# Ten gathered attention tiles: one value product each in place of two, and another set of constants for the order

## The chip, the cores and the metric

The kernel runs on one core of a Trainium2 chip. The metric is the device time of one execution in microseconds (us); lower is better. A measurement of this kernel is the median of several executions. Beside these there is a profile of one execution, with the start and the duration of each instruction on each engine.

The engines are TensorE (PE, with its weight loads as PEld), VectorE (DVE), ScalarE (ACT), GpSimd (POOL) and SyncE (SP). SP's queue carries most of the DMA transfers.

## The reference

Sparse attention over `B, H, S, D = 4, 8, 768, 64`, followed by a feed-forward layer of 512 to 2048 to 512 with a squared ReLU:

```python
scores = scale * np.matmul(q, k.transpose(0, 1, 3, 2))
mask = np.abs(blk_i - blk_j) <= 1            # blocks of 32 positions, 24 of them
mask = mask | (blk_i == 0) | (blk_j == 0) | (blk_i == n_blocks - 1) | (blk_j == n_blocks - 1)
...                                          # and three sampled key blocks for each query block
attn = softmax(np.where(mask, scores, -1e9))
x = np.matmul(attn, v)                       # heads side by side: 3072 x 512
r = np.maximum(x @ w_in, 0.0)
out = (r * r) @ w_out
```

The first and the last query block see all keys; each other block sees its neighbours, the two edge blocks and its three sampled blocks.

## The kernel before

Everything lies in one program without loops. Python functions issue the instructions of single steps, and a planner inside the kernel decides, when the program is built, in which order they are issued.

**Batches 0 and 1** are computed densely, with a mask. A unit is a pair of heads (four units for each batch). Q and K come in as f32, are cast to bf16 (`cast_qk`), transposed by PE (`transp`, `transp_pe`) and copied to `QK` (`evac`, with the helper `copy` at L289 and L291). A score visit (`scores`, L513 and L517) uses half of the array's rows for each head. Then follow `exps` on ACT (L524), the mask product on DVE (`masks`, L531), the value products (`values`, L553), `normalize`, a transpose back (L570) and a copy into `xT`.

**Batches 2 and 3** are computed in gathered tiles, six for each batch, in the order `SEQ` = 5, 0, 1, 2, 3, 4. A tile holds four blocks of queries (tile 5 holds two, and beside them the two edge blocks that see all keys). Keys are gathered by DVE and ACT copies within SBUF. Values are written to DRAM (`vd`) and come back as a window (`v_window`, SP, L704) and as sampled blocks (`v_random`, POOL's indirect DMA, L714) into one of two buffers, which the profile names `RAW` and `MK` after the memory that they share. For each tile of four blocks there are two scores (`s_scores`, L726), one for each pair of head pairs, two `s_exps` (L738), and then the value products (`s_values`, L772), which write 32-row strips of one accumulator `ab`. `s_normalize`, `s_transp` (L788) and `s_evac` bring the result into `xT`.

**The feed-forward layer** runs beside the attention. `hidden` (L821) multiplies `xT` by `w_in`; `relu` (ACT L830 or DVE L832) and `square` (POOL L843 or ACT L841) give `g`; `output` (L871) multiplies by `w_out`; `out_copy` and `store` write the result.

**The order.** Each step is a `Task` with the engines that may run it, an estimated duration, the tasks that it depends on, the buffers that it takes (`get`) and frees (`put`), a key, and a time `after` before which the planner doesn't start it. `run_schedule` always takes the task that can start first by its own clock, and among equals the one with the lowest key. A small pseudo-random number, drawn from `SEEDS` and scaled by `TIES`, is added to each key. Tasks with keys of 100 and more (the feed-forward layer, casts for later batches, gathered tiles that are late in the list) may go ahead of a key under 100 on the same engine only where they could start more than `AHEAD` sooner. The due times come from these constants:

- `PACE0`, `PACE` and `VISITS`: the score visits of batch 1, one entry of `VISITS` for each
- `LEAD`: the casts of Q and K for batch 1, against the visits
- `TILE_AT`: the scores of the twelve gathered tiles; `SLEAD` us before that their gathers may begin
- `EARLY`: the loads of the eight units of batches 2 and 3
- `NB_`: how far the keys of the gathered batches are spread
- `PATIENCE`, `KACT`: how long the planner holds back for a score visit, and how much it prefers DVE for a gather

The scores of all batches, and the value products too, are chained in one fixed sequence, so a due time only counts where it is later than those ahead of it. The planner knows nothing of the chip but its own estimates; what the chip runs is the order of instructions on each engine that comes out.

Of the kernel before, what the change touches and what calls it, by code (L numbers as in the profile page):

```python
# [25 lines left out]
def kernel(  # L26
# [62 lines left out]
    OVER = {"PE": 0.0, "DVE": 0.08, "ACT": 0.09, "POOL": 0.03, "SP": 0.0}  # L89
    SWITCH, HEAD, SLACK = 0.096, 0.14, 0.1  # L90
    SEGMENT, FETCH = 256, 4.6
    AHEAD = {"PE": 0.055, "DVE": 0.075, "ACT": 0.127, "POOL": 0.0, "SP": 0.0}
    LEAD = -4.055
    NB_, SLEAD, KACT = 78.318, 3.363, 0.3
    EARLY = (-37.337, -571.032, -447.965, 102.579, 109.844, 58.537, 96.246, 21.479)
    TILE_AT = (-87.603, 9.262, 99.097, 156.639, -2.44, 142.415, 182.155, 190.828, 133.068, 169.829, 174.13, 84.9)
    VISITS = (8.112, -135.256, -11.672, -92.97, -64.857, -395.022, 12.104, -192.992, -90.327, 19.791, -173.633, -177.084, -46.108, -63.873, -62.087, -15.727, 6.189, 16.892)
    HOLD, PATIENCE = 0, 20.357
    PACE0, PACE, SINGLE, MASK_AT = 45.988, 1.334, 1, 17.0

# [2 lines left out]
    class Buf:  # L105
        def __init__(self, pool):
# [2 lines left out]

    TIES = 2.072, 7.892
    SEEDS = (
            371417, 510513, 591591, 260703, 130052, 619188, 398403, 547159, 30476,
            318629, 58182, 18274, 283039, 791673, 964966, 267641, 668336, 10009,
            208115, 562447, 518448, 450915, 243995, 901117)

# [14 lines left out]
    class Task:  # L134
        def __init__(self, engs, key, fn, deps=(), get=(), put=(), after=0.0, mode=None, dma=0.0, late=None, bias={}, port=False,
# [8 lines left out]
            self.order = len(tasks)  # L144
            self.key += TIES[0 if key < 300 else 1] * tie(self.order)
            for b in self.put:
# [745 lines left out]
    def T_(engs, key, f, *args, **kw):  # L892
        return Task(engs, key, (lambda e: f(*args, e)), **kw)
# [132 lines left out]
    def attend_sparse(b):  # L1026
        us = range(b * HP, (b + 1) * HP)
        keys = [ev[u][1, 0] for u in us]
        qrs = [ev[u][0, 0] for u in us]
        vals = [x for u in us for x in cv[u]]  # L1030
        base = N1 + (b - ND) * NB_
        wr = T_(("SP", 0.6), base - 5, vd_write, b, deps=vals + sp0, dma=2.1)
        xs_first = True
        for p_ in range(NT):
            t = SEQ[p_]
            n = len(blocks_of(t))
            seq = STILES.index((b, p_))
            x = seq % 2
            s = base + p_ * NB_ / NT
            kb, vb = Buf("KG"), Buf("VG")  # L1040
            over = {0: lambda: [y for u in range(ND * HP) if raw_set(u) == 2 for y in cv[u] + tr[u]], 1: lambda: []}[x]() if seq < 2 else []
            vover = ([y for u in range(ND * HP) if raw_set(u) == 3 for y in cv[u] + tr[u]] if x == 0 else mks) if seq < 2 else []
            deps = []
            late = TILE_AT[seq]
            if p_ in PLACES:
                ts = SEQ[p_:PLACES[p_]]
                kp = T_(("DVE", 1.5), s - 8.1, k_places, ts, deps=sp0 + k_last[-1:], after=late - SLEAD - 2.0)
            k1 = T_({"DVE": 0.43, "ACT": 0.61}, s - 8, k_window, b, t, x, list(range(n))[:2], deps=keys + over + k_first[-1:], get=[kb],
                    after=late - SLEAD, port=True, nop=2, bias={"ACT": KACT})
            deps.append(k1)  # L1050
            k_first.append(k1)
            if n > 2:
                deps.append(T_({"DVE": 0.43, "ACT": 0.61}, s - 8, k_window, b, t, x, [2, 3], deps=[k1], port=True, nop=2, bias={"ACT": KACT}))
            if p_ < 2:
                deps.append(T_(("DVE", 0.8 if p_ == 0 else 0.49), s - 8, k_global, b, x, p_ == 0, deps=[k1] + kg_all[-1:], port=True, nop=2))
                kg_all.append(deps[-1])
            for qs_ in ([0, 1], [2, 3])[:n // 2]:
                deps.append(T_(("DVE", 1.2), s - 8, k_random, b, t, x, qs_, deps=[k1, kp] + sp0, port=True, nop=6))
            k_last.append(deps[-1])
            deps.append(T_({"DVE": 0.6, "POOL": 1.27}, s - 8, q_tile, b, t, x, deps=qrs + [k1] + qz, after=late - SLEAD, port=True, nop=2))  # L1060
            v1 = T_(("SP", 1.1), s - 8, v_window, b, t, x, deps=[wr] + vover + v_first[-1:], get=[vb], dma=0.38 * n, after=late - SLEAD)
            vdeps = [v1]
            v_first.append(v1)
            if p_ < 2:
                vdeps.append(T_(("SP", 1.8), s - 8, v_global, b, x, deps=[v1], dma=1.0))
            for i in range(n):
                vdeps.append(T_(("POOL", 1.05), s - 8, v_random, b, t, x, i, deps=[v1] + sp0, dma=0.48, late=5.5, quiet=True))
            pairs = [(0, 1), (2, 3)] if n == 4 else [(a,) for a in range(HP)]
            ab = Buf("X2")
            va = None  # L1070
            groups = [[g_] for g_ in pairs] if n == 4 else [pairs[0:2], pairs[2:4]]
            for k_, grp in enumerate(groups):
                end = k_ == len(groups) - 1
                us_sc, nm_ = (0.47, 16) if n == 4 else (0.46, 10)
                exs, pts = [], []
                for j, g_ in enumerate(grp):
                    sb_ = Buf("X2")
                    sc = T_(("PE", us_sc), s, s_scores, b, t, x, g_, sb_, deps=deps + sc_all[-1:], get=[sb_],
                            put=[kb] if end and g_ == grp[-1] else [], mode=128, after=late, paced=True, mm=nm_)
                    sc_all.append(sc)  # L1080
                    pt = Buf("pT")
                    pts.append(pt)
                    ex = T_(("ACT", 1.02), s, s_exps, b, t, g_, deps=[sc], get=[pt], put=[sb_])
                    if t in (0, NT - 1):
                        ex = T_({"DVE": 0.09 * len(g_), "POOL": 0.15 * len(g_)}, s - 1, s_patch, b, t, g_, deps=[ex])
                    exs.append(ex)
                    for u in us:
                        sc_of[u].append(sc)
                va = T_(("PE", 0.245 if n == 4 else 0.5), s + 2.6 * NB_ / 36, s_values, b, t, x, grp, ab, deps=exs + vdeps + va_all[-1:],
                        get=[] if k_ else [ab], put=pts + ([vb] if end else []), mode=32, mm=32 if n == 4 else 64)  # L1090
                va_all.append(va)
                for u in us:
                    va_of[u].append(va)
            xb_ = Buf("xs")
            nm = T_(("DVE", 0.95), s - 9, s_normalize, b, t, deps=[va], get=[xb_])
            kw = {}
            if b not in xb:
                xb[b] = Buf("xT")
                kw = dict(get=[xb[b]])
            xt = T_(("PE", 0.24), s - 9, s_transp, b, t, deps=[nm], put=[xb_], mode=128, mm=4)  # L1100
            mu["s", b, p_] = T_({"DVE": 0.47, "ACT": 0.56}, s - 9, s_evac, b, t, p_, deps=[xt], put=[ab], **kw)
# [4 lines left out]
    sc_all, va_all, ob = [], [], {}  # L1106
    mr = []
    for i, (c0, c1) in enumerate(((0, QW), (QW, S))):
        rb_ = Buf("X1")
        t = T_(("PE", 0.11 + 0.11 * i), 5.0 if i else -90.0, mask_rows, c0, c1, rb_, after=9.8 if i else 4.6, get=[rb_], put=[], mode=32, mm=1)  # L1110
# [6 lines left out]
    for us in [range(b * HP, (b + 1) * HP) for b in range(B)]:  # L1117
# [8 lines left out]
        if us[0] < HP:  # L1126
            for c0, c1, at in MASKED:
                for n in range(NCH):
                    mb, w = Buf("X1"), (c1 - c0) / 512
                    t = T_(("PE", 0.216 * w), (2 * n + 30 if c0 == 0 else 2 * n + 2), mask_tile, n, c0, c1, mb, get=[mb], mode=128, after=at, deps=mr, mm=1)  # L1130
                    x = T_({"DVE": 0.15 + 0.53 * w, "ACT": 0.22 + 0.37 * w}, (2 * n + 30 if c0 == 0 else 2 * n + 2), mask_evac, n, c0, c1, deps=[t], put=[mb])
                    for c in range(c0, c1, P):
                        mk[n, c] = x
        while mine:
            n = min(len(mine), GROUPS[us[0] // HP][mine[0][1] // QW])
            if n == 3:
                n = sum(a[:2] == mine[0][:2] for a in mine)
# [8 lines left out]
    for k_, T in enumerate(TILES + [None]):  # L1146
# [4 lines left out]
        for _, kind, x in sorted(both, key=lambda z: z[:2]):  # L1151
            n_key += 1
            t = x[0]
            b, c0, w = t
            if kind == 0:
# [9 lines left out]
                for part in range(parts):  # L1165
                    end = part == parts - 1
                    hd.append(T_(("PE", HID[w] / parts), n_key - (0.6 if part else 0.5), hidden, t, f, part, parts, hb,
                                 deps=hd[-1:] or need + [wl[f * NWP // NF], wl[(f + per_unit(t) - 1) * NWP // NF]],
                                 get=[] if part else [hb], put=[xb[b]] if last_use and end else [], mode=128, mm=per_unit(t) * KM // parts, yields=not part and pool == "X2"))
# [3 lines left out]
                n = 1 if wide else per_unit(t)  # L1173
# [3 lines left out]
            else:  # L1177
                _, i, part = x
                ts, cs = y_tiles(t)[i]
                n = (cs[1] - cs[0]) / d_model  # L1180
                fs = range(part * NF // NY, (part + 1) * NF // NY)
                if part == 0:
# [3 lines left out]
                        deps=[sq_of[t, f] for f in fs] + [wl[NWP + f * NWP // NF] for f in fs] + ([yprev] if part else []),  # L1186
                        get=[] if part else [yb], put=[gbuf[t, f] for f in fs if (t, f) in gbuf] if last_i else [], mode=128, mm=NF // NY)
# [39 lines left out]
```

## Time and profile before

| | |
|---|---|
| median of 3 runs | 271.44 us (271.15 to 272.69) |
| the profiled execution | 271.15 us, of which 269.2 are the profile's span |
| busy share of the span | PE 96%, ACT 74%, DVE 60%, POOL 54% |
| granted TensorE clock | full, mean 1.00 |
| data read from HBM and written to it | 37.62 MB and 8.03 MB |

The profiled time is the time of the whole execution; the span runs from the first to the last instruction that the profile shows. All times of instructions below are counted from the start of the span. "L871" is line 871 of the kernel, "x16" is a count of instructions, and an entry such as `[0.16 <-issue]` tells how long the engine stood idle just before a group and what ended that. The "chain that ended last" is followed back from the last instruction: at each step to what released it, or to the instruction before it on its engine.

### The profile page before, as it was taken

The page shows a single profiled execution, that of the slowest core. Times are in us where ns is not written, and L with a number is a line of the kernel's source. Part 1 is how long each engine was busy: PE and PEld are TensorE (multiplying, and loading weights), DVE is VectorE, ACT ScalarE, POOL GpSimd, SP SyncE. Part 2 cuts the span into 40 slices and gives each one's busy share as a digit, 9 for nine tenths or more (in the row PEclk, how much of TensorE's full clock was granted, in tenths as well). Part 3 has the DMA queues.
Part 4 walks back from the last instruction along what each step waited for, and adds up shares of the span by engine and source line. Part 5 has one row for each costly group of instructions (what it writes and reads, how often), then busy time and mean ns, then how long its engine had stood idle before and what let it go on. Part 6 is the DMA issues. An engine that isn't in the chain of part 4 may idle for free.

```text
span 269.2 us, 8933 instructions
## 1 busy us (share of the span) xinstructions
PE 259.4 (96%) x3658; PEld 170.6 (63%) x3696; DVE 161.2 (60%) x465; ACT 199.9 (74%) x304; POOL 146.4 (54%) x185
## 2 busy tenths in 40 slices
PE   8999999989999999999999999999999999999995
PEld 6778876667676746665766556655675666545544
DVE  7898898989898689899535464361444723301010
ACT  3897989988989799888975549845878876714821
POOL 4292915765971410468886771762288975712520
PEclk9999999999999999999999999999999999999999
DMA  6999999955511025669769681326453372321022
GB/s 204 373 259 205 205 225 313 348 176 178 175 41 52 1 73 184 178 228 208 191 196 284 226 211 43 104 80 207 106 128 103 95 207 67 104 70 38 0 80 78
DMA packets 39184, 42.04 MB, mean 156 GB/s; under 512 B 2888, under 2 KB 34536, under 8 KB 39144
## 3 DMA queue, kind: packets, MB, share of 16 engines
q1 hardware_dynamic: 32264, 32.29, 39.2%
q0 software_dynamic: 6336, 8.79, 16.2%
q8 instruction: 29, 0.48, 0.7%
q10 hardware_dynamic: 544, 0.39, 0.5%
q14 instruction: 11, 0.09, 0.1%
HBM read 37.62 MB, written 8.03 MB: 170 GB/s over the span
## 4 chain that ended last, share of the span: by engine, by line
PE 79%; DVE 9%; ACT 4%; issue 3%; POOL 3%; ACTq 0%
PE py L871 25%; PE X L821 24%; PE X L513 5%; PE po L553 5%; DVE pT L531 4%; PE X L772 3%; PE X L726 3%; PE F L821 3%; ACT pT L524 2%; PE X L471 2%; PE X L871 2%; ACT r L830 1%; POOL g L843 1%; PE po L570 1%; PE F L360 1%
## 5 line engine op out<-in xcount | busy, mean ns | idle before, releaser
L843 POOL TENSOR_TENSOR g<-r 128x384 bf16<-128x384 f32 (+1 forms) x65 | 60.6, 946 | 82.4 <-ACT r L830 69.7
L871 PE MATMUL py<-w_out_sb,g 128*128 128x512 bf16 (+2 forms) x346 | 84.2, 367 | 3.1 <-issue 1.0
L821 PE MATMUL X<-xT,w_in_sb 128*128 128x384 bf16 (+1 forms) x512 | 86.7, 313 | 0.1
L524 ACT ACTIVATE pT<-X 128x1024 bf16<-128x1024 f32 (+1 forms) x76 | 70.6, 985 | 6.3 <-PE X L513 4.0
L821 PEld LDWEIGHTS <-w_in_sb 128*128 128x128 bf16 x640 | 54.8, 98 | 25.8 <-issue 1.1
L830 ACT ACTIVATE r<-X 128x768 f32<-128x768 f32 (+1 forms) x58 | 43.4, 761 | 20.1 <-PE X L821 17.8
L871 PEld LDWEIGHTS <-g 128*128 128x128 bf16 x416 | 36.4, 98 | 30.2 <-POOL g L843 1.0
L531 DVE TENSOR_TENSOR pT<-pT,MK 128x1024 bf16<-128x1024 bf16 x60 | 48.3, 821 | 5.4 <-ACT pT L524 5.1
L738 ACT ACTIVATE pT<-X 128x1024 bf16<-128x1024 f32 x28 | 27.4, 1034 | 5.2 <-PE X L726 4.8
L841 ACT ACTIVATE g<-r 128x384 bf16<-128x384 f32 (+1 forms) x55 | 28.4, 537 | 1.9 <-DVE r L832 0.9
L553 PEld LDWEIGHTS <-pT 128*128 128x128 bf16 x576 | 22.5, 97 | 7.1 <-issue 2.3
L513 PE MATMUL X<-QK 64*128 64x256 bf16 (+1 forms) x336 | 25.5, 257 | 0.9 <-ACT QK L289 0.7
L553 PE MATMUL po<-VN,pT 128*128 128x65 bf16 x576 | 25.8, 193 | 0.3 <-DVE pT L531 0.2
L714 POOL DMA_INDIRECT MK<-vd,idx x24 | 22.4, 934 | 6.4 <-issue 4.7
L289 ACT COPY ys<-py 128x512 f32<-128x512 f32 (+1 forms) x17 | 9.8, 578 | 17.7 <-PE py L871 17.7
L714 POOL DMA_INDIRECT RAW<-vd,idx x20 | 18.8, 942 | 5.5 <-issue 4.4
L780 DVE RECIPROCAL rss<-X 128x8 f32<-128x8 f32 x12 | 2.5, 207 | 31.4 <-PE X L772 29.6
L513 PEld LDWEIGHTS <-QK 64*128 64x128 bf16 x336 | 13.7, 94 | 11.1 <-issue 8.4
L291 POOL CAST VN<-RAW 128x768 bf16<-128x768 f32 x15 | 15.5, 1039 | 8.3 <-DMA RAW<-in_v_dram 8.2
L832 DVE TENSOR_SCALAR r<-X 128x768 f32<-128x768 f32 (+1 forms) x6 | 5.5, 912 | 23.3 <-PE X L821 17.8
L291 DVE CAST qc<-RAW 128x768 bf16<-128x768 f32 (+3 forms) x24 | 16.0, 683 | 0.0
L291 POOL CAST qc<-RAW 128x768 bf16<-128x768 f32 (+2 forms) x11 | 11.9, 1099 | 0.6 <-DMA RAW<-in_q_dram 0.6
(113 smaller groups left out, 295.4 us busy)
## 6 DMA issues: line engine op xcount, KB each, us to landing
RAW<-in_v_dram SPq DMA_DIRECT2D x16, 384.0 KB, 6.4
RAW<-in_k_dram SPq DMA_DIRECT2D x15, 384.0 KB, 4.9
out_dram<-ys SPq DMA_DIRECT2D x21, 256.0 KB, 2.2
RAW<-in_q_dram SPq DMA_DIRECT2D x12, 384.0 KB, 3.7
MK<-vd SPq DMA_DIRECT2D x12, 204.0 KB, 3.9
w_in_sb<-in_moe_w_in_dram POOLq DMA_DIRECT2D x4, 512.0 KB, 6.9
w_out_sb<-in_moe_w_out_dram POOLq DMA_DIRECT2D x4, 512.0 KB, 17.2
vd<-VN SPq DMA_DIRECT2D x2, 816.0 KB, 4.1
```

Source lines behind the costliest of these rows:

```text
L291: (V if e == "DVE" else G).tensor_copy(out=out, in_=in_)
L513: nc.tensor.matmul(ps[:, h, j * w:(j + 1) * w], QK[i][hs, 1, ksl], QK[i][hs, 0, qsl], start=j == 0, stop=not add, skip_group_check=True)
L524: A.activation(out=pT[:, :, 0:n], in_=stile.pop(a)[:, :, 0:n], func=AF.Exp, scale=scale)
L531: V.tensor_tensor(out=pT, in0=pT, in1=m[:, None].broadcast_to([P, 2, len(cs), w]), op=AOP.mult)
L553: nc.tensor.matmul(po[:, qc, h, :], pT[:, h, j * w + qc * P:j * w + (qc + 1) * P], VT[i][:, n, h, 0:VW], start=(n == 0 and qc == 0 and h = ...
L714: G.indirect_dma_start(out=VG[x][0:96, i, 1, :], out_offset=None, in_=vd[b][:, :], in_offset=bass.IndirectOffsetOnAxis(ap=idx[:, n:n + 1], ...
L738: A.activation(out=pT, in_=stile.pop((b, t, s_)), func=AF.Exp, scale=scale)
L821: nc.tensor.matmul(htile[T, f][:, i], w_in_sb[:, kc, (f + i) * P:(f + i + 1) * P], xT[b][:, kc, c0:c0 + w], start=(kc == 0), stop=(kc == K ...
L830: A.activation(out=to, in_=src, func=AF.Relu)
L841: A.activation(out=g, in_=r, func=AF.Square)
L843: (G if e == "POOL" else V).tensor_mul(out=g, in0=r, in1=r)
L871: nc.tensor.matmul(ytile[T, i], gtile[T, f][:, ts * P:(ts + 1) * P], w_out_sb[:, f, cs[0]:cs[1]], start=(f == 0), stop=(f == NF - 1))
```

## The change

Two things change. In tiles of four blocks the two pairs of heads now form one group: both scores and both exps come first, and one `s_values` task of 64 matmuls depends on both, where two tasks of 32 stood, one behind each exp. And the planner gets another set of constants and another list of seeds, so that the order on all engines is drawn anew.

```diff
-    AHEAD = {"PE": 0.055, "DVE": 0.075, "ACT": 0.127, "POOL": 0.0, "SP": 0.0}
-    LEAD = -4.055
-    NB_, SLEAD, KACT = 78.318, 3.363, 0.3
-    EARLY = (-37.337, -571.032, -447.965, 102.579, 109.844, 58.537, 96.246, 21.479)
-    TILE_AT = (-87.603, 9.262, 99.097, 156.639, -2.44, 142.415, 182.155, 190.828, 133.068, 169.829, 174.13, 84.9)
-    VISITS = (8.112, -135.256, -11.672, -92.97, -64.857, -395.022, 12.104, -192.992, -90.327, 19.791, -173.633, -177.084, -46.108, -63.873, -62.087, -15.727, 6.189, 16.892)
-    HOLD, PATIENCE = 0, 20.357
-    PACE0, PACE, SINGLE, MASK_AT = 45.988, 1.334, 1, 17.0
+    AHEAD = {"PE": 0.072, "DVE": 0, "ACT": 0.016, "POOL": 0.0, "SP": 0.0}
+    LEAD = -1.965
+    NB_, SLEAD, KACT = 98.482, 2.913, 0.3
+    EARLY = (-111.056, -528.755, -508.598, 101.849, 102.656, 86.28, -118.551, 2.902)
+    TILE_AT = (-122.17, 115.286, 17.571, 152.206, 17.119, 136.102, 178.344, 190.091, 79.428, 180.052, 142.791, 19.732)
+    VISITS = (3.261, -138.646, -28.394, -72.627, -42.286, -382.173, 18.638, -143.108, -87.499, 16.494, -192.092, -177.045, -34.569, -53.721, -84.242, -11.105, -9.629, 16.057)
+    HOLD, PATIENCE = 0, 11.991
+    PACE0, PACE, SINGLE, MASK_AT = 45.309, 1.36, 1, 17.0
...
-    TIES = 2.072, 7.892
+    TIES = 1.974, 9.683
...
-            groups = [[g_] for g_ in pairs] if n == 4 else [pairs[0:2], pairs[2:4]]
+            groups = [pairs] if n == 4 else [pairs[0:2], pairs[2:4]]
...
-                va = T_(("PE", 0.245 if n == 4 else 0.5), s + 2.6 * NB_ / 36, s_values, b, t, x, grp, ab, deps=exs + vdeps + va_all[-1:],
-                        get=[] if k_ else [ab], put=pts + ([vb] if end else []), mode=32, mm=32 if n == 4 else 64)
+                va = T_(("PE", 0.48 if n == 4 else 0.5), s + 2.6 * NB_ / 36, s_values, b, t, x, grp, ab, deps=exs + vdeps + va_all[-1:],
+                        get=[] if k_ else [ab], put=pts + ([vb] if end else []), mode=32, mm=64)
```

The 24 numbers of `SEEDS` are replaced as well.

More of the change, by code (lines that the diff above doesn't have):

```diff
@@ L107, in __init__ @@
             self.pool, self.holds, self.free, self.at = pool, 0, 0.0, None
-    TIES = 2.072, 7.892
+    TIES = 1.974, 9.683
     SEEDS = (
-            371417, 510513, 591591, 260703, 130052, 619188, 398403, 547159, 30476,
-            318629, 58182, 18274, 283039, 791673, 964966, 267641, 668336, 10009,
-            208115, 562447, 518448, 450915, 243995, 901117)
+            338909, 700375, 826346, 372260, 127050, 184109, 927138, 534498, 372383,
+            383233, 219274, 236594, 48969, 494981, 466408, 463984, 717825, 205211,
+            929930, 623139, 563588, 438717, 508538, 442750)
     def tie(n):
```

## The prediction

> **What bounds the kernel now.** I read the page from the top: busy shares, then the chain that ended last, then PE's own waits, then busy time by stage, and last the order of instructions around each place that the diff touches.
>
> The page's shares of busy time and the head of its chain:
>
> ```profile
> PE 259.4 (96%) x3658; PEld 170.6 (63%) x3696; DVE 161.2 (60%) x465; ACT 199.9 (74%) x304; POOL 146.4 (54%) x185
> ```
>
> ```profile
> PE 79%; DVE 9%; ACT 4%; issue 3%; POOL 3%; ACTq 0%
> ```
>
> PE is busy for 259.4 of 269.2 us, and it carries 79% of the chain. Of the 9.8 us that it stands idle, 1.2 lie before its first matmul and 3.3 behind its last (it starts at 265.7), so about 5 us are gaps inside. The change removes no matmul, so PE's work stays. Only gaps and boundaries can move.
>
> PE's own waits, longest first (line waited for: total us, times, longest):
>
> ```profile
> PE F L360 <- DVE bm L342: 1.2, 1, 1.2
> PE py L871 <- issue: 1.0, 6, 0.2
> PE X L513 <- ACT QK L289: 0.7, 1, 0.7
> PE py L871 <- POOL g L843: 0.7, 2, 0.5
> ```
>
> No wait is long. From the start times of the matmuls I took what each step between two starts has beyond the usual step of its form (0.216 us for 512 columns). Pauses over 0.2 us, apart from the changes of array shape: 0.60 us at 21.3, 0.88 at 56.0, 0.46 at 61.8, 0.41 at 71.5, 0.33 at 73.3, 0.23 at 89.7 and 0.67 at 206.7, together **3.6 us**. That is about all that a better order could win back. Five of the seven lie between 56 and 90 us, so I asked for busy time there (stage, then span, PE, PEld, DVE, ACT, POOL with instructions, clock, DMA share, GB/s):
>
> ```profile
> 40.00:54.00 14.00, 13.84 (x177) 8.97 (x176) 13.20 (x28) 13.65 (x19) 8.56 (x8) 1.00 0.98 331
> 54.00:75.00 21.00, 19.44 (x278) 14.20 (x279) 18.76 (x39) 18.03 (x26) 14.09 (x12) 1.00 0.56 173
> 75.00:96.00 21.00, 20.63 (x245) 14.34 (x248) 16.87 (x37) 18.44 (x27) 10.16 (x9) 1.00 0.07 25
> ```
>
> Here, where batch 0's attention ends and batch 1's opens, PE, DVE and ACT are all nearly full, and PE loses 1.56 us between 54 and 75. The clock is granted in full throughout, so it is no term of the sum.
>
> The Trainium skill, "Perfetto Trace Analysis", section "Identifying the Most-Contended Engine", would judge TensorE's headroom by LDWEIGHTS busy time and calls matmul busy time a bad measure. By that, 63% would leave a third of the span, some 99 us (estimate), to a better order. The starts say otherwise: 37 matmuls of 512 columns in 8.15 us from 177.4 on, with nothing between them. The sum goes by the starts.
>
> **Part 1: one value product in place of two.** Ten gathered tiles have four blocks each, and each had two `s_values` tasks of 32 matmuls. The timeline shows how they run:
>
> ```profile
> 170.97 0.69 PE L772 MATMUL X<-MK,pT 128*32 128x65 bf16 x64
> 175.05 0.69 PE L772 MATMUL X<-RAW,pT 128*32 128x65 bf16 x64
> 241.49 0.69 PE L772 MATMUL X<-MK,pT 128*32 128x65 bf16 x64
> 242.34 1.24 PE L871 MATMUL py<-w_out_sb,g 128*128 128x512 bf16 x5 [0.16 <-issue]
> ```
>
> In all ten cases the two halves stand back to back as 64. The step across the seam is at most 20 ns where a usual one is 3 or 4. Merging saves 10 x 0.016 = 0.16 us at most. What it adds is a wait of the first half for the second exp. That exp ended 6 us or more before the product in every tile (tile at 241.49: exps ended by 224.2), so it costs nothing. Were that cover gone, the first half (about 0.3 us) would move behind the second exp, 10 x 0.3 = 3 us at the most, and only if PE had no other work, while feed-forward matmuls stand around all ten. The accumulator and the score tiles are taken and freed where they are now. **0 us** (-0.2 to +0.3).
>
> The Trainium skill, "TensorE: Matmul & The Clock Gate", section "The mechanism", has LDWEIGHTS overlapping running matmuls only where the row group differs. Taken strictly, each of the 896 loads of these products (94 ns) would stand exposed, 84 us (estimate). The row has 64 products in 0.69 us, so here the loads overlap.
>
> **Part 2: changes of array shape.** A step from 64-row scores (L513) to 128-row work is 0.166 us longer than the usual step in nearly every one of some 30 places. The grouping of the scores is not in the diff, so the number of visits stays. Another order can put a few more or fewer side by side: **0 us**, +-0.7 (four visits).
>
> **Part 3: the opening of batch 1.** Worked out from the constants: its first score visit was due at 54.1 and becomes due at 48.6; the casts for it were due at 50.0 and become due at 47.3. In the trace this visit stands at 56.99, 2.9 behind its due time, released by a copy of QK.
>
> ```profile
> 53.10 0.55 DVE L291 CAST qc<-RAW 128x768 bf16<-128x768 f32 x1
> 55.57 0.54 DVE L291 COPY QK<-X 128x768 bf16<-128x768 bf16 x1
> 56.99 0.61 PE L513 MATMUL X<-QK 64*128 64x256 bf16 x8 [0.72 <-ACT QK L289]
> ```
>
> It can come about 3 us sooner, no more. Drawn forward onto DVE: two casts (18 at a mean of 0.757, 1.5 us), one QK copy (0.55), two mask products of about 0.69 (1.4), 3.45 us. Between 40 and 54 DVE has 0.8 us free. So about 2.6 us of batch 0's masks and normalizations come later, and with them the values and x that PE takes. The chain there ran over DVE already (start, us):
>
> ```profile
> 47.44 4.50 DVE pT L531 x4
> ```
>
> Between 40 and 54 PE lost only 0.16 us although DVE was full: ready feed-forward matmuls covered it. Between 54 and 75 it lost 1.56 in 21. So the price lies between a gain (the waits at 56.0 and 61.8 close, -1.3) and the whole displaced 2.6. I take half of the upper end, **+1.3 us**, since the pauses there show that the cover holds only in part.
>
> The visit that was due at 74.9 becomes due at 81.1. Two exps (1.03 each) and two masks move into a stage with 2.6 us of ACT and 4.1 us of DVE free in 21: **+0.2 us** (-0.4 to +0.6). The load of unit 12 is due 7 us sooner (109.8 to 102.7). It stands on SP's queue ahead of stores and gathers' windows, but the DMA engines are under 0.6 busy there: 0, at worst one store held back, +0.7.
>
> **Part 4: the gathered batches and the end.** The fourth tile's due time goes from 156.6 to 152.2, the first tile of batch 3 from 182.2 to 178.3; the next stays near 190. PE was full on both sides, so coming earlier only trades places with feed-forward work: 0. At the end order matters. The last tile's chain:
>
> ```profile
> 225.94 2.06 SPq L704 DMA_DIRECT2D MK<-vd  x2
> 234.63 0.92 POOL L714 DMA_INDIRECT MK<-vd,idx  x1 [0.30 <-issue]
> 244.50 5.69 PE L821 MATMUL X<-xT,w_in_sb 128*128 128x384 bf16 x34
> ```
>
> Its buffer came free at 225.2, the gathers left POOL by 235.6 and landed some 3.8 later at 239.4; the product ran at 241.5, so 2.1 us were spare. The final hidden products began at 244.5, 0.2 behind the copy of x. Earlier due times leave this slack as it is or add to it: **0 us** (-0.5 to +2.8).
>
> **The sum.** Made against the profiled execution: 269.2 span, 271.15 in all. 271.15 + 0 + 0 + 1.3 + 0.2 + 0 = 272.65. The median of the runs is 0.29 above the profiled one, so **272.9 us**.
>
> **Rivals.** *The orders are worth the same*: the feed-forward matmuls cover the displaced DVE work as between 40 and 54, pauses stay near 3.6: 271.4, within 0.8 of it. For it: between 67 and 256 us PE is idle for 3.6 us of 189; against: the thin cover from 54 to 75.
> *Faster*: with Q and K of batch 1 there 3 us sooner, the waits at 56.0, 61.8, 71.5 and 73.3 (2.1 us) close, and the one for POOL's square at 206.7 goes too: 271.4 - 1.3 to 271.4 - 2.8, about 269.4. It decides once ready feed-forward work covers all of DVE's 2.6 us. Against it: those stages have no free engine.
> *The last tile comes late*: the product at 187.3 to the next on the same buffer at 208.4 took 21.1 us, later laps 16.8 and 16.3. One such long lap at the end costs 4.8 - 2.1 = 2.8 us beside the forecast's: 275.7. It decides when the last product stands more than 2 us behind the end of ready work.
>
> **How the numbers follow.** Forecast's case (271.9 to 275.0) 0.44, the same 0.28, faster 0.18, late last tile 0.10. About 0.5% (1.36 us) is what a measurement of this kernel can tell from no change. Slower: 0.10 + 0.44 less the 0.05 of it under 272.8 = 0.49. Same: 0.28 + 0.05 = 0.33. Faster: 0.18. The range goes from 269.8, which leaves half of the faster case out, to 276.0, which leaves the worst of the last tiles out.
>
> **What would show it.** Right: ten groups of 64 products as before; the first batch 1 scores at 53 to 55 us; PE's busy time within 1 us of 259.4 and its idle time 1 to 2 us larger, with the growth between 47 and 75 us; the last hidden products begin where they did, plus that. Wrong: PE's pauses shrink there, or the time lies elsewhere: behind a late last tile, in more changes of shape, or in longer matmuls.

## The result, and the profile after

| | before | after |
|---|---|---|
| median of 16 runs each | 271.28 us (270.68 to 272.69) | 273.77 us (272.85 to 275.24) |
| profiled execution, its span | 271.15, 269.2 | 273.77, 271.7 |

The ratio is 1.0088 [1.0072, 1.0104]: slower by 2.5 us, against 272.9 predicted. (Four of the experiments below fell on a chip that granted less clock from 134 us on; they are read up to there, not by their times.)

Busy time and the head of the chain that ended last, of the kernel after:

```profile
PE 260.8 (96%) x3659; PEld 171.0 (63%) x3696; DVE 165.2 (61%) x463; ACT 200.9 (74%) x308; POOL 148.9 (55%) x183
...
PE 85%; DVE 10%; issue 1%; ACT 1%; POOL 0%; DVEq 0%; ACTq 0%
```

DVE has 4.0 us more busy time, although the change gives it no work. The 60 mask products (L531) account for 3.6 of it: 48.3 us before, 51.9 after. PE's own waits after (line waited for: total us, times, longest) have a new one at their head:

```profile
PE po L570 <- DVE xq L563: 1.5, 1, 1.5
PE F L360 <- DVE bm L342: 1.2, 1, 1.2
PE X L471 <- POOL qc L291: 0.6, 1, 0.6
PE X L513 <- ACT pT L524: 0.5, 1, 0.5
```

Busy time in stretches of the kernel after (stretch, span, PE, PEld, DVE, ACT, POOL with instructions, clock, DMA share, GB/s):

```profile
54.00:75.00 21.00, 19.14 (x255) 13.62 (x257) 20.40 (x36) 18.40 (x26) 15.34 (x14) 1.00 0.56 165
75.00:96.00 21.00, 20.37 (x239) 13.97 (x240) 19.34 (x43) 16.31 (x24) 9.88 (x10) 1.00 0.09 30
94.00:108.00 14.00, 13.08 (x177) 7.57 (x179) 12.86 (x28) 13.30 (x16) 1.04 (x1) 1.00 0.23 74
```

and the last stretch in the kernel before:

```profile
94.00:108.00 14.00, 13.89 (x164) 7.78 (x165) 12.03 (x25) 13.44 (x15) 1.28 (x2) 1.00 0.39 124
```

PE loses more in 54 to 75 us, as forecast, and also in 94 to 108, where it had lost next to nothing. The last matmul starts at 268.16 us, 2.44 later than before. Summing what each step between two matmul starts has beyond the usual step of its form, after minus before: -0.47 us up to 40; **+1.45 from 40 to 67**; +0.08 to 94; **+1.47 from 94 to 108**; +0.1 to 134; +0.27 to 148; -0.69 from there to the end; +0.2 in the usual steps themselves. Another choice of the usual step moves each of these sums by up to 0.5 us; the two large ones stay. So there are two places to explain.

The first is seen in the timeline of the kernel after (start, us, engine, line, operation, tiles, count, idle time before and its releaser):

```profile
61.65 4.80 DVE L531 TENSOR_TENSOR pT<-pT,MK 128x1024 bf16<-128x1024 bf16 x4
66.58 0.42 DVE L563 TENSOR_TENSOR xq<-po,rs 128x256 bf16<-128x256 f32 x1
```

```profile
62.16 1.29 POOL L291 CAST VN<-RAW 128x768 bf16<-128x768 f32 x1
63.40 2.52 POOL L291 CAST qc<-RAW 128x768 bf16<-128x768 f32 x2
65.86 1.28 POOL L291 CAST VN<-RAW 128x768 bf16<-128x768 f32 x1
```

```profile
67.06 0.28 PE L570 MATMUL po<-identb,xq 128*128 128x128 bf16 x2 [1.47 <-DVE xq L563]
```

Four mask products in a row take 4.80 us. Three of them take 1.30 us each, where a mask alone takes 0.68. GpSimd casts beside them from 62.16 on. Behind the masks stands the normalization `xq` of batch 1's first unit, and PE waits for it. In the order before, that normalization stood ahead of two of these four masks, and three of the four took 0.67 to 0.69 us each (the first, at 62.21, 0.76):

```profile
63.83 0.67 DVE L531 TENSOR_TENSOR pT<-pT,MK 128x1024 bf16<-128x1024 bf16 x1
65.88 1.28 DVE L531 TENSOR_TENSOR pT<-pT,MK 128x1024 bf16<-128x1024 bf16 x2
```

### The profile page after: what moved, and what is told of

Its sections match the earlier page's. It is cut to its first block, busy times and chain, and to the rows that moved or that the text cites. A ratio compares the mean times of both kernels' runs of the same rounds, so it can differ in the third digit from the quotient of the medians.

```text
span 271.7 us, 8945 instructions
## 1 busy us (share of the span) xinstructions
PE 260.8 (96%) x3659; PEld 171.0 (63%) x3696; DVE 165.2 (61%) x463; ACT 200.9 (74%) x308; POOL 148.9 (55%) x183
## 4 chain that ended last, share of the span: by engine, by line
PE 85%; DVE 10%; issue 1%; ACT 1%; POOL 0%; DVEq 0%; ACTq 0%
PE py L871 26%; PE X L821 26%; DVE pT L531 7%; PE X L513 6%; PE po L553 6%; PE X L726 4%; PE X L772 4%; PE F L821 3%; PE X L471 2%; PE X L871 2%; DVE QK L291 2%; PE F L460 1%; PE F L360 1%; PE po L570 1%; PE X L788 1%
## 5 line engine op out<-in xcount | busy, mean ns | idle before, releaser
L843 POOL TENSOR_TENSOR g<-r 128x384 bf16<-128x384 f32 (+1 forms) x64 | 60.2, 951 | 87.4 <-ACT r L830 71.4
L821 PE MATMUL X<-xT,w_in_sb 128*128 128x384 bf16 (+1 forms) x512 | 88.2, 313 | 0.7 <-ACT QK L289 0.5
L871 PE MATMUL py<-w_out_sb,g 128*128 128x512 bf16 (+2 forms) x347 | 86.4, 367 | 2.5 <-issue 1.0
L821 PEld LDWEIGHTS <-w_in_sb 128*128 128x128 bf16 x640 | 55.4, 98 | 29.6 <-issue 2.2
L830 ACT ACTIVATE r<-X 128x768 f32<-128x768 f32 (+1 forms) x55 | 42.0, 765 | 27.1 <-PE X L821 26.7
L531 DVE TENSOR_TENSOR pT<-pT,MK 128x1024 bf16<-128x1024 bf16 x60 | 51.9, 892 | 1.0 <-ACT pT L524 0.8
L513 PE MATMUL X<-QK 64*128 64x256 bf16 (+1 forms) x336 | 26.1, 257 | 0.7 <-ACT pT L524 0.5
L289 ACT COPY ys<-py 128x512 f32<-128x512 f32 (+1 forms) x20 | 11.6, 579 | 11.1 <-PE py L871 11.1
L291 DVE CAST qc<-RAW 128x768 bf16<-128x768 f32 (+3 forms) x23 | 16.9, 746 | 0.1
L289 ACT COPY QK<-X 128x768 bf16<-128x768 bf16 x13 | 10.2, 803 | 6.5 <-DVE QK L291 5.7
L291 POOL CAST qc<-RAW 128x768 bf16<-128x768 f32 (+2 forms) x12 | 12.6, 1059 | 1.0 <-DMA RAW<-in_q_dram 0.6
```

What stands on the lines that cost most here:

```text
L291: (V if e == "DVE" else G).tensor_copy(out=out, in_=in_)
L513: nc.tensor.matmul(ps[:, h, j * w:(j + 1) * w], QK[i][hs, 1, ksl], QK[i][hs, 0, qsl], start=j == 0, stop=not add, skip_group_check=True)
L531: V.tensor_tensor(out=pT, in0=pT, in1=m[:, None].broadcast_to([P, 2, len(cs), w]), op=AOP.mult)
L821: nc.tensor.matmul(htile[T, f][:, i], w_in_sb[:, kc, (f + i) * P:(f + i + 1) * P], xT[b][:, kc, c0:c0 + w], start=(kc == 0), stop=(kc == K ...
L830: A.activation(out=to, in_=src, func=AF.Relu)
L843: (G if e == "POOL" else V).tensor_mul(out=g, in0=r, in1=r)
```

## The experiments

**Theories.** *Collision*: the new order puts GpSimd's casts and DVE's masks side by side between 60 and 67 us; each slows the other, DVE falls behind, PE waits. *Due times*: the visit moved to 81.1 us packs later exps and masks into 94 to 108. *Merge*: the larger value product costs the time. *Late constants*: the due times of the loads and of the gathered batches cost it, through later transfers.

Where a kernel below has "its own order written out", the planner is replaced by a list of the tasks, engines and banks that it had chosen, so that an edit leaves all else in place:

```diff
-    run_schedule({"PE": 4.4, "DVE": 4.4, "ACT": 3.65, "POOL": 3.7, "SP": 16.0}, ...)
+    for w_ in ORDER.split():          # 18A 24G 19P4 21D 25P5 ...: task, engine, bank
+        ...
+        t.fn(e)
```

**merge_alone.** The merge put into the kernel before, with tasks numbered as before.

```diff
-            groups = [[g_] for g_ in pairs] if n == 4 else [pairs[0:2], pairs[2:4]]
+            groups = [pairs] if n == 4 else [pairs[0:2], pairs[2:4]]
```

> The kernel before with the merged value product alone (numbers of the pseudo-random draw kept, so that no other key changes). Theory A (the constants and seeds make the whole loss): ten groups of 64 products as before, 271.3 us within 0.4. Rival (the merge costs by itself, through later value products): 272 us or more, with gaps around L772.

Measured 271.26 us (270.73 to 272.75), ratio 1.0001 [0.9984, 1.0017]. The order on every engine is that of before. The merge costs nothing that can be measured (the interval leaves 0.5 us either way); the difference comes with the order.

**short_casts.** The order after written out; three of GpSimd's casts write a sixth of their columns and one, K of unit 8, a third. The other columns of these four keys and values are left out of the computation.

```diff
-        copy(e, VT[u][:, :, :, 0:D], raw[u][2].rearrange("p t n d -> p n t d"))
+        copy(e, *((y[:, 0:1] if e == "POOL" and u in (8, 9) else y) for y in (VT[u][:, :, :, 0:D], raw[u][2]...)))
...   # likewise K of units 6 and 8
```

> The kernel after with its own order written out as a list, and four casts on POOL (V of units 8 and 9, K of units 6 and 8) that write a sixth of their elements; nothing else is changed. Theory A (POOL's casts beside the mask products slow DVE, and so x comes late to PE at 65 us): the four masks that took 1.1 to 1.3 us each from 61.7 on take about 0.7, PE's wait of 1.5 us for xq goes, 272.3 to 272.9 us. Rival (the score visits simply stand too dense there for DVE): the wait stays above 0.8 us and the time at 273.5 or more.

Measured 272.17 us (271.09 to 274.71), ratio 1.0041 [1.0013, 1.0068]. Its DVE and GpSimd in the same place:

```profile
61.06 2.56 DVE L531 TENSOR_TENSOR pT<-pT,MK 128x1024 bf16<-128x1024 bf16 x3
63.85 0.69 DVE L531 TENSOR_TENSOR pT<-pT,MK 128x1024 bf16<-128x1024 bf16 x1 [0.22 <-ACT pT L524]
```

```profile
61.58 0.75 POOL L291 CAST VN<-RAW 128x128 bf16<-128x128 f32 x1
62.28 1.61 POOL L291 CAST qc<-RAW 128x128 bf16<-128x128 f32 x2
```

The same four masks end 64.5 - 61.1 = 3.4 us after the first began, not 4.8; PE's pause of 1.63 us shrinks to 0.31, and 1.6 us of the 2.5 are gone by the medians. The runs spread from 271.09 to 274.71 us, and the ends of the two intervals leave anything from 0.1 to 2.5 us for the gain, so the starts of matmuls further below are the better measure of it.

**normalize_first.** The order after with the normalization moved one mask ahead.

> The kernel after with its own order written out, and on DVE alone the normalization of unit 4's first half of queries stands ahead of the fourth mask instead of behind it. Theory A (the wait of 1.5 us at 65 us is DVE's order on a late queue): the wait falls to 0.2 to 0.5, 272.5 to 273.0 us. Rival (the masks are needed as urgently): the wait moves to the value products behind, and the time stays at 273.5 or more.

Measured 273.78 us (273.31 to 273.98), ratio 1.0085 [1.0066, 1.0103]. The transpose now waits 0.41 us, but the waits of PE have moved on:

```profile
PE X L471 <- POOL qc L291: 1.2, 1, 1.2
PE po L553 <- DVE xT L291: 0.9, 1, 0.9
```

The second row is the wait that followed, at 67.9 us; the first stands at 133.6, far behind the edit. Which step stands behind the slowed masks makes no difference; DVE as a whole is late. The rival was right.

**seventh_due_back.** The due time of the seventh visit as in the kernel before, the rest as after.

```diff
-    VISITS = (3.261, -138.646, -28.394, -72.627, -42.286, -382.173, 18.638, ...)
+    VISITS = (3.261, -138.646, -28.394, -72.627, -42.286, -382.173, 12.445, ...)
```

> The kernel after with one constant changed, the seventh entry of VISITS, so that this visit of batch 1 is due at 74.9 as before and not at 81.1. Theory A (the visits behind it are packed until ACT holds PE up at 102 us): the visits stand 2.5 us or more apart from 94 to 108, PE loses 1 to 1.5 us less there, and with the rest of the order drawn anew 272 to 273.3 us. Rival (any order that is not searched as a whole is worse): 274 us or more, whatever that stretch shows.

Measured 276.85 us (275.94 to 278.51), ratio 1.0203 [1.0173, 1.0233]. The planner redrew much of the order. The seventh visit came 4.3 us sooner (80.62 against 84.95), but the visits behind it stood as dense as in the kernel after, and PE was idle for 0.79 of the 14 us from 94 to 108 (0.92 after, 0.11 before). The first pause stayed too, 1.63 us at 67.2. So this due time alone does not cause the loss. Visits further apart, which the expectation had asked for, did not come about, and what they would be worth is not shown.

**copy_first.** In the order after, a copy of the output bank on DVE is moved ahead of five masks, and two output products ahead of the scores behind it, to fill PE's pauses there.

> The kernel after with its own order written out and one output tile moved: on DVE its copy out of PSUM goes ahead of five mask products at 99 us, on PE the two output steps that need the freed bank go ahead of the next score visit. Theory B (between 98 and 104 us the visits stand 1.2 to 2 us apart, ACT's exps hold the score banks, and PE has no feed-forward work because the output bank is copied out late): PE's gaps of 0.3, 0.3 and 0.8 us there shrink by 0.6 to 0.9 in all, 272.9 to 273.3 us. Rival (the masks behind the copy come late by as much): the gap moves to the value products, 273.6 or more.

Measured 274.35 us (273.61 to 275.81), ratio 1.0116 [1.0091, 1.0141]. The pauses moved: they are 0.81 us at 102.5 and 0.54 at 105.9 now. (One of 0.58 us at 94.9 lies ahead of the edit; the profiles of *short_casts* and *short_exps* have it as well, and that of after has not.) The rival was right here too.

**three_waits.** The order before, with feed-forward products moved ahead of two of PE's waits, and a gathered tile's value product ahead of a third.

> The kernel before with its own order written out, and on PE alone ready feed-forward matmuls moved ahead of the instructions that waited at 56.0 (0.88 us) and 61.8 (0.46), and the gathered tile's value product ahead of the output step that waited at 206.7 (0.67). If such pauses are worth their length: 269.3 to 269.9 us. If the engines behind PE's order set the pace there and the wait only moves on: 270.8 to 271.4.

Measured 273.67 us (272.36 to 274.95), ratio 1.0078 [1.0057, 1.0099]: slower. The pause at 56.0 us is gone, and others have come:

```profile
PE X L772 <- ACT r L830: 2.1, 1, 2.1
PE F L360 <- DVE bm L342: 1.2, 1, 1.2
PE X L471 <- DVE qc L291: 1.2, 1, 1.2
```

The row of L360 stands in the kernel before too; the other two are new. Filling the first gap only brought PE to another wait, 1.2 us for a cast of DVE. The wait of 2.1 us is that of the value product which was moved: it could not run yet where it now stands. In the profile the granted clock was 0.50 from 211.3 to 214.7 us, just behind that wait; but four of the six executions had 0.999 or more and still took 272.36 to 273.92 us.

**late_constants_in_before** and **late_constants_back.** The constants of the gathered batches and of the loads exchanged: after's in the kernel before (with the merge), then before's in the kernel after.

```diff
-    NB_, SLEAD, KACT = 78.318, 3.363, 0.3
-    EARLY = (-37.337, -571.032, ...)
-    TILE_AT = (-87.603, 9.262, ...)
+    NB_, SLEAD, KACT = 98.482, 2.913, 0.3
+    EARLY = (-111.056, -528.755, ...)
+    TILE_AT = (-122.17, 115.286, ...)
```

> The kernel before with the merge and with after's EARLY, TILE_AT, NB_, SLEAD (loads and gathered tiles of batches 2 and 3); the rest as before, so the order is the same up to 75 us. If the loss lies in the opening and the end of batch 1 alone: 271 to 272 us. If a set of constants is only good as a whole: 273 us or more, with the loss behind 75 us.

Measured 280.13 us (279.29 to 281.62), ratio 1.0330 [1.0296, 1.0363], with one wait that the profile puts down to a load:

```profile
PE py L871 <- DMA RAW<-in_v_dram: 3.7, 1, 3.7
```

> The kernel after with EARLY, TILE_AT, NB_ and SLEAD of before. The wait of 1.5 us at 65 us stays. If the loss lies in the opening and the end of batch 1: 273.3 to 274.5 us. If a set of constants is only good as a whole: 275 us or more.

Measured 274.51 us (273.71 to 275.18), ratio 1.0127 [1.0105, 1.0149]; the first pause stays, 1.63 us at 64.9. The two do not agree. In the kernel before, the foreign half cost 8.8 us; behind the wait of 3.7 us the granted clock was 0.50 from 132.3 to 139.1 us, in a place where the kernel after has no such wait. In the kernel after it cost 0.7, at the edge of what was expected if the loss lies in the opening and the end of batch 1. What both show is that the late constants alone are not the cause: with those of before the loss stays.

**The last four: a control for the casts, and ScalarE in 94 to 108 us.** *short_casts_before* makes the same cut as *short_casts* in the order before. The others halve six exponentials; the mask products behind these read the mask itself as their first input, so the weights there are not those of the reference:

```diff
-        A.activation(out=pT[:, :, 0:n], in_=stile.pop(a)[:, :, 0:n], func=AF.Exp, scale=scale)
+        m = n // 2 if a[0] in (4, 5) and a[1] == 512 else n; A.activation(out=pT[:, :, 0:m], ...)
```

> The kernel before, its own order written out as a list, with the same four of GpSimd's casts (V of units 8 and 9, K of units 6 and 8) writing a sixth of their columns; the rest of the columns of these four keys and values is left out of the computation. It is the control of the run short_casts. Theory (the collision of casts and mask products between 60 and 69 us belongs to the new order: in the order before, the masks of 54 to 69 us took 0.68 to 0.76 us each): next to nothing to gain, 270.8 to 271.5 us, ratio 0.998 to 1.001, while the same cut took 1.6 us from the kernel after. Rival (less work on GpSimd helps any order as much): 269.7 us, ratio 0.994, and then the collision explains nothing of the difference between the two kernels.

> The kernel after, its own order written out as a list, with the six exponentials of units 4 and 5 over the queries from 512 on (those from about 96 to 103 us) taken over half their columns; the mask products behind them take the mask itself as their first input, so these products' weights are not those of the reference. That takes about 6 x 0.43 = 2.6 us from ScalarE where it is busy 13.3 of 14 us (94 to 108). Theory A (ScalarE's row of exponentials sets the pauses of 102 to 104 us): the time beyond the matmuls' own pace in 94 to 108 us falls from 4.4 to about 3 us, the pause of 0.77 us at 102.9 goes, 272.3 us in all, ratio 1.003 to 1.005. Theory B (DVE's masks and copies, or the few ready feed-forward products in that stretch, set it; ScalarE is busy beside them): the pauses move by less than 1 us and the time stays at 273.4 to 274.0 us, ratio 1.008 to 1.010.

> The two cuts together in the order of the kernel after (four casts of GpSimd at a sixth, six exponentials at half; what they leave out is as in the two runs alone). Theory A (two separate costs, one in 60 to 69 us and one in 94 to 108): the gains add, 1.6 + 1.5 = 3.1 us, 270.7 us, ratio 0.997 to 0.999. Theory B (the second stretch is not ScalarE's): 272.0 to 272.4 us as with the casts alone, ratio 1.003 to 1.005.

> The two cuts together in the order of the kernel before, as the control of short_both. Theory (that order has neither cost: PE was busy 6.95 of 7 us in each half of 94 to 108 us): 270.6 to 271.4 us, ratio 0.997 to 1.000. Rival (the order before pays for ScalarE's row too, 12 exponentials in 11.55 us from 93.9): 269.7 us or less, ratio below 0.995, and the second stretch is then no difference of the two orders in what they wait for.

On that chip the kernel before took 299.56 us (296.70 to 303.24), and the ratios were 1.0053 [1.0002, 1.0104], 1.0543 [1.0479, 1.0607], 1.0328 [1.0253, 1.0403] and 1.0065 [1.0010, 1.0119]. No expectation in microseconds of the whole can be judged by these. Up to 134 us the clock is granted in full, though, and PE runs the same matmuls in the same order as the kernel that each was made from. So I compare the start of the same score product in each (us later than in the profile of its own parent, after or before):

| | ahead of the four casts (63 to 68 us in the parent) | behind them (79 to 85) | behind the six exps (109 to 114) |
|---|---|---|---|
| short_casts (after) | -0.58 | -2.36 | -1.78 |
| short_exps (after) | +1.48 | +1.47 | +2.06 |
| short_both (after) | -0.21 | -1.99 | -1.40 |
| merge_alone (before) | +0.14 | +0.14 | +0.13 |
| short_casts_before | +0.91 | +0.75 | +0.75 |
| short_both_before | +0.16 | 0.00 | +0.01 |

*The casts.* In the order after the cut wins 1.78 us, twice the same; in the order before, 0.16 us, twice the same. (There two of the four casts lie ahead of the first column, from 60.58 us on; the starts at 56.99, ahead of all four, are later by the same 0.91 and 0.16.) Of the 1.78, 1.33 are there by 69 us, at the pause itself. The collision belongs to the new order, as expected; the rival, that less GpSimd work helps any order, is out.
*The exps.* Between the last two columns *short_both* loses 0.59 us, exactly as *short_casts* does with its exponentials whole (a pause of the transposes near 92 us, absent from the profiled execution of after); in the order before the cut wins nothing either. The theory that ScalarE's row sets the pauses of 94 to 108 us fell, although ScalarE was busy for 13.3 of 14 us there. With the exps halved the waits pass to DVE (*short_both*):

```profile
100.91 0.28 PE L570 MATMUL po<-identb,xq 128*128 128x128 bf16 x2 [0.19 <-DVE xq L563]
...
102.31 0.87 PE L553 MATMUL po<-VN,pT 128*128 128x65 bf16 x23 [0.57 <-DVE xT L291]
```

DVE's row of masks, normalizations and copies is one candidate that remains: 12.86 of 14 us busy after, 12.03 before. Another is that PE has less to fill its gaps with: 23 feed-forward matmuls start or run there after, 36 before. Neither was tested. The collision of casts and masks is not it: GpSimd is busy for 1.04 of these 14 us, and all masks but one take 0.68 or 0.69. So this second place is narrowed down, not settled.

## Why the prediction held, step by step

The chain that it named was the right one, and its range held. That its terms lie as near to the measured ones as they do is in part luck, as the parts below show.

**What bounds the kernel.** Right. PE's busy time rose by 1.4 us, its idle time from 9.8 to 10.9. The forecast had at most 1 us and 1 to 2 us, so only the split between the two was a little off.

**Part 1, the merge: 0.** Right, by *merge_alone*. The step of 18 to 20 ns at the seam of each product is still there, so not even the 0.16 us were saved. (The 896 loads named there are those of all twelve tiles; the ten have 640, which makes 60 us by the same estimate in place of 84.) The ten products stand as groups of 64 as before, here two of them:

```profile
168.43 0.69 PE L772 MATMUL X<-MK,pT 128*32 128x65 bf16 x64
172.37 0.69 PE L772 MATMUL X<-RAW,pT 128*32 128x65 bf16 x64
```

**Part 2, changes of array shape: 0 +-0.7.** Right: the steps from scores to 128-row work add up to 7.6 us both before and after.

**Part 3, the opening of batch 1: +1.3.** The size was near, +1.45 in 40 to 67 us, and so was the chain: DVE late, PE waiting behind it. The size was luck, since the working was wrong in three points. The first visit came 1.3 us sooner, not 3, and not between 53 and 55:

```profile
55.69 0.61 PE L513 MATMUL X<-QK 64*128 64x256 bf16 x8
```

Its due time is not what moved it: put back alone, in either kernel, it leaves the planner's list of every engine as it is. What was late was batch 1's own first normalization, not batch 0's masks. And DVE was not late from 3.45 us of work drawn forward. From 54 to 75 us its busy time grew by 1.64 us (18.76 to 20.40), while the masks' time beyond 0.68 us each grew from 1.44 to 4.41 us there. So the lengthening alone exceeds the growth. The step that failed is the price of a mask product: I took 0.69 us for each, and the trace of before already held masks of 1.30 us beside casts (71.1 and 72.3 us) that I did not price. Nor is it casts alone: the mask at 55.96 took 1.53 us beside two of GpSimd's squares (L843, at 55.48 and 56.91).

The Trainium skill, "SBUF — State Buffer", section "Who interferes with whom", states this: a VectorE instruction with two inputs in SBUF contends with a GpSimd instruction that reads SBUF, over a pair of ports that the two engines share as an exclusive lock. The rows agree in the main. Masks (62.69, 63.92, 65.15) and casts (62.16, 63.40, 64.63, 65.86) go in turns: each begins some 1.23 us after the last of its kind, where a mask alone takes 0.68 us and a cast that meets no mask 0.82 (at 69.79 in the kernel before). One after the other the two would take 1.50, so they still overlap by 0.27, which is less strict than a lock for the whole instruction. A cast cut to a sixth takes 0.75 us beside these masks, and 0.29 where it meets none (*short_casts_before*, at 70.70).

The planner in this kernel does price such a meeting: `run_schedule` notes in `port` when DVE and GpSimd were last at work, and lengthens the later step (`p1 - r + us - HEAD`). With its 0.68 for a mask, 0.83 for a cast of V and 0.14 for `HEAD`, a pair that meets comes to 1.23 us, as measured. My sum had no such term. Whether two steps meet, the planner judges by its own clock, not by the chip's.

**Part 3, the seventh visit: +0.2.** The term that was mis-sized: 94 to 108 us lost 1.47 us. Its cause is not the due time by itself (*seventh_due_back*) and not ScalarE's free time, by which I had sized it (*short_exps*, *short_both*).

**Part 4, the tail: 0.** Right; from 148 us on PE won 0.69 us. The last tile's product ran 3.2 us sooner than before, and the last hidden products did too:

```profile
238.31 0.69 PE L772 MATMUL X<-MK,pT 128*32 128x65 bf16 x64
...
241.33 3.09 PE L821 MATMUL X<-xT,w_in_sb 128*128 128x384 bf16 x18
```

I had expected these to begin where they did, plus the loss ahead; that sign of being right did not come. They are not tied to the end: PE was full behind them, so the end came from the sum of PE's pauses alone.

**The sum.** 1.3 + 0.2 = 1.5 us forecast, 2.5 measured. Of the 2.5, the cut of the casts takes back 1.6 by the medians (1.78 by the starts, against 0.16 in the control). The remaining 0.9 fits the 1.47 us of the second place less the 0.69 won at the end, which is an account and not an experiment.

**The rivals.** *The same worth* fell: PE's pauses over 0.2 us, without the changes of shape, sum to some 5.3 us after, 3.6 before. *Faster* fell on the condition that I gave it: feed-forward products did not cover DVE's delay. *A late last tile* did not happen.

## What to carry to other kernels

A sum that prices each instruction alone can't see that two engines slow each other: look in the trace for one operation with two durations, and for what runs beside the longer one, before its mean goes into a sum. Where the kernel has a planner, read what it prices. When a row of instructions on one engine is late, moving a single step in it only passes the wait on; take the load off the row and see whether PE moves. And an engine that is busy for 95% of a stretch is a suspect, not a cause: halving ScalarE's work there gave PE nothing.

## What the runs showed of the hardware that was not expected

On the chip of the last four runs PE paused between its own small products with nothing that released it ("issue"): steps of 0.69 to 0.72 us and twice that. *short_casts_before*, stretches and PE's waits:

```profile
0.00:134.00 134.00, 128.30 (x1749) 89.36 (x1766) 112.94 (x265) 114.52 (x162) 68.76 (x91) 1.00 0.69 189
134.00:180.00 46.00, 38.29 (x560) 23.50 (x563) 16.66 (x79) 22.78 (x37) 22.37 (x30) 0.93 0.53 150
```

```profile
PE X L772 <- issue: 5.2, 8, 1.2
PE py L871 <- issue: 5.0, 8, 3.6
```

In this run the pauses began at 135 us, and the granted clock fell to one half for the first time at 154.3, for 3.4 us; so the clock did not start them here. In the kernel before on the other chips there is no such wait at L772. The two kernels with the order after lost 3 to 5% there, the two with the order before under 1%. Why the orders differ so much in this, no run tells.
